# One small SBUF tile made 64 bytes wider, in a channel attention and rational feed-forward kernel

## The chip, the cores and the metric

The kernel runs on one core of a Trainium2 chip. The metric is device time in microseconds (us), from one execution of the program; several runs are compared by their median.

## The reference

There are 4 batches of 6080 tokens with 256 channels. The first part is an attention over channels, the second a feed-forward layer whose activation is a quotient of two polynomials:

```python
qn = q / (norm(q, axis=1) + 1e-06)            # q, k, v: (4, 6080, 256), norms over the tokens
kn = k / (norm(k, axis=1) + 1e-06)
s  = kn.transpose(0, 2, 1) @ qn / tau         # (4, 256, 256)
a  = exp(s - s.max(-1)); a /= a.sum(-1) + 1e-09
x  = (v @ a).reshape(24320, 256)
h  = x @ w_in                                 # w_in: (256, 2048)
P  = a0 + a1*h + a2*h**2 + a3*h**3
Q  = 1 + abs(b0)*abs(h) + abs(b1)*h**2
out = (P / (Q + 1e-06)) @ w_out               # w_out: (2048, 256)
```

All is float32.

## The kernel before

The attention matrix of a batch is multiplied into w_in once per batch (`fuse`), so that each token needs two products only: `mm1`, from the 256 channels of v to the hidden units, and `mm2`, from the hidden units to 256 outputs. To keep float32 accuracy, each operand is split into a high and a low part, and each product is the sum of three: high by high, high by low, low by high.

Tokens are worked on in groups of 512, the last group of a batch has 448. The 2048 hidden units are cut into 8 pairs of 2 x 128. For one group and one pair (`pair`), mm1 is two runs of 6 matmuls: `whi` by `vhi`, `whi` by `vlo`, `wlo` by `vhi` for each half of the 256 channels, into one bank of the PSUM tile `hx`. ACT, DVE and POOL make the rational function of hx out of it with `d`, `uu` and `r`, in two parts `ghi` and `glo` (tiles `gh`, `gl`). mm2 then multiplies these with `w_out_hi` and `w_out_lo` and adds into the PSUM tile `acc`, 12 matmuls per group and pair. In the profile a matmul is written as output, stream and weights: `hx<-vhi,w` streams vhi past the weights in w. The low weights have the tiles `w2`, which the profile's names show as `w` too.

Beside that PE makes the products of k and q of the next batch (`hx<-kq`, `acc<-kq`) and the fused weights (`hx<-w_in_sb,kq`), both in plain float32, where one product is two matmuls in the profile.

Each engine's instructions stand in an order that a planner (`Planner`) works out when the kernel is built, from costs and from the due times in `LAG` and `TIME`. The addresses play no part in it.

Tiles in SBUF are made at the end, once all sizes are known: `buf` notes the greatest size of each tag in `homes`, and the loop over `homes.items()` (L1140 to L1144) makes the tiles in the order in which the tags were first used. In the built program they lie one after the other, each rounded up to 32 bytes per partition. Six of them are very small: n2, e, rn, st and two of sm, 16 bytes each, so 32 with rounding. They lie between orow and w:

| tiles, in this order | bytes of one | start before | residue of 128 |
|---|---|---|---|
| w_in_sb, w_out_hi, w_out_lo | 16384 | 17888 (first) | 96 |
| d, uu, r, kq, sq, orow | 4096 | 67040 (first) | 96 |
| n2, e, rn, st, sm, sm | 16 | 132576 (n2) | 96, 0, 32, 64, 96, 0 |
| w (8), w2 (8) | 2048 | 132768 (first) | 32 |
| vst, vhi, vlo | 4096 | 165536 (vst) | 32 |
| sacc | 2048 | 186016 | 32 |
| ssq, gh, gl | 4096 | 188064 (ssq) | 32 |

So mm1 has its weights and its streams at residue 32, and mm2 has weights at residue 96 and streams at 32. All offsets of the operands inside these tiles are multiples of 512 bytes.

Of the kernel before, what the change touches and what calls it, by code (L numbers as in the profile page):

```python
# [297 lines left out]
def tile_channel_attention_rational_ffn(  # L298
# [841 lines left out]
    for tag, width in homes.items():  # L1140
        if tag in ("hA", "hB"):
            continue
        home, n = (ps, SLOTS["hA" if tag == "hx" else tag]) if tag in ("hx", "acc") else (sb, SLOTS[tag])
        homes[tag] = [home.tile([P, width], F32, name=f"{tag}{i}") for i in range(n)]  # L1144
    for s in plans[0][1]:
        s.fn()
# [39 lines left out]
```

## Time and profile before

| | us |
|---|---|
| median of 3 runs | 2421.33 (2420.75 to 2424.07) |
| profiled execution, its own time | 2420.11 |
| its span, first to last instruction | 2418.2 |
| PE busy | 2370.3 |
| DVE busy | 2156.7 |
| ACT busy | 2067.5 |
| POOL busy | 1839.3 |

All times of instructions below come from the profiled execution. A matmul's length in the profile is longer than the distance to the next one's start, since matmuls overlap; how long PE needs per matmul is read from the distance of starts.

### The profile page before, as it was taken

How to read it: one execution, taken by the hardware profiler on the slowest of the kernel's cores; microseconds unless marked ns; L12 is line 12 of the kernel's file. 1: busy time of each engine (PE TensorE's matmuls, PEld its weight loads, DVE VectorE, ACT ScalarE, POOL GpSimd, SP SyncE). 2: the span in 40 equal slices, each digit the busy share in tenths (PEclk: the TensorE clock that was granted, in tenths of full speed). 3: DMA queues.
4: the chain of work that ended last, by engine and by line, in shares of the span. 5: the costliest groups of instructions: out<-in, count | busy, mean ns of one | idle time of the engine just before them, and what ended most of it. 6: DMA issues, size and time to landing. Idle time of an engine off the chain costs nothing.

```text
span 2418.2 us, 30382 instructions
## 1 busy us (share of the span) xinstructions
PE 2370.3 (98%) x10312; PEld 1938.8 (80%) x10312; DVE 2156.7 (89%) x2627; ACT 2067.5 (85%) x2072; POOL 1839.3 (76%) x1427
## 2 busy tenths in 40 slices
PE   7899999999999999999999999999998999999998
PEld 5677888888888888888888888888887788888887
DVE  5889999997878799999987889999996999999998
ACT  4789999986767799999986689999997999999996
POOL 7797777778779977777768987777774777777775
PEclk9899999999999999999999999999999999999999
DMA  9532121136467511211146731211111121111201
GB/s 299 159 71 36 18 36 18 18 57 150 87 142 152 119 26 22 31 18 28 25 89 140 169 61 23 30 18 28 24 18 18 20 33 18 27 27 18 32 12 19
DMA packets 455862, 141.15 MB, mean 58 GB/s; under 512 B 395888, under 2 KB 445040, under 8 KB 455696
## 3 DMA queue, kind: packets, MB, share of 16 engines
q1 hardware_dynamic: 447152, 108.04, 21.6%
q0 software_dynamic: 8544, 31.07, 7.2%
q8 instruction: 83, 1.36, 0.2%
q14 instruction: 83, 0.68, 0.1%
HBM read 83.10 MB, written 24.90 MB: 45 GB/s over the span
## 4 chain that ended last, share of the span: by engine, by line
PE 89%; ACT 4%; DVE 2%; issue 2%; DMA 2%; POOL 1%; SPq 0%; DVEq 0%; ACTq 0%; POOLq 0%
PE hx L83 47%; PE acc L83 42%; ACT d L83 2%; ACT r L83 1%; DVE hx L83 1%; ACT uu L83 1%; SPq L83 0%; DVE orow L83 0%; DMA vst<-in_v_dram 0%; DMA d<-in_moe_w_in_dram 0%; DVE gl L83 0%; DVE gh L83 0%; DMA d<-in_q_dram 0%; DMA kq<-in_q_dram 0%; DMA kq<-in_k_dram 0%
## 5 line engine op out<-in xcount | busy, mean ns | idle before, releaser
L83 POOL TENSOR_TENSOR d<-d,gh 128x512 f32<-128x512 f32 (+1 forms) x768 | 978.1, 1303 | 418.7 <-DVE gh L83 414.9
L83 PE MATMUL hx<-vhi,w 128*128 128x512 f32 (+1 forms) x3072 | 1052.6, 391 | 3.8 <-DVE gl L83 2.9
L83 PEld LDWEIGHTS hx<-vhi,w 128*128 128x128 f32 x3072 | 577.5, 188 | 131.5 <-DVE gl L83 5.7
L83 DVE SCALAR_TENSOR_TENSOR hx<-hx,fast,d 128x512 f32<-128x512 f32 (+1 forms) x768 | 566.2, 745 | 61.3 <-POOL d L83 60.2
L83 PE MATMUL hx<-vlo,w 128*128 128x512 f32 (+1 forms) x1536 | 600.1, 391 | 0.0
L83 ACT ACTIVATE uu<-hx,fast 128x1024 f32<-128x1024 f32 (+1 forms) x384 | 422.7, 1101 | 155.5 <-PE hx L83 155.3
L83 POOL TENSOR_SCALAR d<-d,ones,fast 128x1024 f32<-128x1024 f32 (+1 forms) x384 | 467.5, 1220 | 109.6 <-ACT r L83 103.1
L83 DVE TENSOR_TENSOR gl<-hx,r 128x512 fp32r<-128x512 f32 (+1 forms) x768 | 518.1, 678 | 32.7 <-PE acc L83 5.3
L83 DVE SCALAR_TENSOR_TENSOR gh<-hx,fast,r 128x1024 fp32r<-128x1024 f32 (+1 forms) x384 | 485.7, 1265 | 58.1 <-ACT r L83 48.9
L83 DVE SCALAR_TENSOR_TENSOR hx<-uu,fast,hx 128x1024 f32<-128x1024 f32 (+1 forms) x384 | 487.6, 1270 | 35.8 <-ACT d L83 19.6
L83 PE MATMUL acc<-gh,w_out_hi 128*128 128x512 f32 (+1 forms) x1536 | 487.6, 399 | 5.9 <-DVE gh L83 3.3
L83 PE MATMUL acc<-gl,w_out_hi 128*128 128x512 f32 (+1 forms) x1536 | 481.5, 395 | 1.8 <-DVE gl L83 1.8
L83 PE MATMUL acc<-gh,w_out_lo 128*128 128x512 f32 (+1 forms) x1536 | 479.4, 393 | 0.0
L83 ACT ACTIVATE d<-hx 128x1024 f32<-128x1024 f32 (+1 forms) x384 | 387.5, 1009 | 78.6 <-PE hx L83 76.3
L83 ACT ACTIVATE r<-d,fast 128x1024 f32<-128x1024 f32 (+1 forms) x384 | 438.9, 1144 | 11.0
L83 ACT ACTIVATE r<-r 128x1024 f32<-128x1024 f32 (+1 forms) x384 | 403.5, 1052 | 8.3
L83 ACT ACTIVATE d<-d 128x1024 f32<-128x1024 f32 (+1 forms) x384 | 403.3, 1051 | 7.1
L83 PEld LDWEIGHTS acc<-gh,w_out_hi 128*128 128x128 f32 x1536 | 285.8, 188 | 79.2 <-DVE orow L83 16.4
L83 PEld LDWEIGHTS acc<-gl,w_out_hi 128*128 128x128 f32 x1536 | 288.6, 188 | 67.4 <-DVE gl L83 3.4
L83 PEld LDWEIGHTS acc<-gh,w_out_lo 128*128 128x128 f32 x1536 | 289.2, 188 | 65.8
L83 PEld LDWEIGHTS hx<-vlo,w 128*128 128x128 f32 x1536 | 288.7, 188 | 63.5
L83 PE MATMUL hx<-kq 128*128 128x256 f32 (+1 forms) x592 | 137.0, 386 | 12.7 <-DVE fast L83 7.4
(118 smaller groups left out, 1120.9 us busy)
## 6 DMA issues: line engine op xcount, KB each, us to landing
ssq<-sq POOLq DMA_DIRECT2D x54, 512.0 KB, 5.2
vst<-in_v_dram SPq DMA_DIRECT2D x176, 128.0 KB, 4.1
out_dram<-orow SPq DMA_DIRECT2D x176, 128.0 KB, 3.4
kq<-in_k_dram SPq DMA_DIRECT2D x75, 256.0 KB, 4.1
kq<-in_q_dram SPq DMA_DIRECT2D x75, 256.0 KB, 4.4
d<-in_moe_w_in_dram SPq DMA_DIRECT2D x8, 512.0 KB, 5.8
ssq<-sq POOLq DMA_DIRECT2D x6, 448.0 KB, 5.3
r<-in_k_dram SPq DMA_DIRECT2D x9, 256.0 KB, 5.6
```

What stands on the lines that cost most here:

```text
L83: ins = op(*args, **kwargs)
```

## The change

The tile n2 gets 16 more float32 elements per partition, 64 bytes. Nothing reads or writes them.

```diff
@@ -1141,6 +1141,8 @@
         if tag in ("hA", "hB"):
             continue
         home, n = (ps, SLOTS["hA" if tag == "hx" else tag]) if tag in ("hx", "acc") else (sb, SLOTS[tag])
+        if tag == "n2":
+            width += 16
         homes[tag] = [home.tile([P, width], F32, name=f"{tag}{i}") for i in range(n)]
     for s in plans[0][1]:
         s.fn()
```

Every tile behind n2 starts 64 bytes later: w at 132832, vst at 165600, ssq at 188128, all at residue 96 of 128, as are the tiles ahead of n2, which stay. Of the small tiles e, rn, st and the two of sm go to 64, 96, 0, 32 and 64. Modulo 64 no tile's start changes. The instructions of every engine and their order are the same as before.

## Rows read from the trace of the kernel before

**Rows 1.** The page: span, busy time, clock, chain that ended last.

```profile
span 2418.2 us, 30382 instructions
PE 2370.3 (98%) x10312; PEld 1938.8 (80%) x10312; DVE 2156.7 (89%) x2627; ACT 2067.5 (85%) x2072; POOL 1839.3 (76%) x1427
...
PEclk9899999999999999999999999999999999999999
...
PE hx L83 47%; PE acc L83 42%; ACT d L83 2%; ACT r L83 1%; DVE hx L83 1%; ACT uu L83 1%; SPq L83 0%; DVE orow L83 0%; DMA vst<-in_v_dram 0%; DMA d<-in_moe_w_in_dram 0%; DVE gl L83 0%; DVE gh L83 0%; DMA d<-in_q_dram 0%; DMA kq<-in_q_dram 0%; DMA kq<-in_k_dram 0%
```

**Rows 2.** That chain in time order: start us, length us, what, instructions.

```profile
1185.09 1.40 PE acc L83 x6
1186.49 1.39 PE hx L83 x6
...
1190.40 2.80 PE acc L83 x12
1193.21 2.75 PE hx L83 x12
```

**Rows 3.** PE groups by shape: what, count | busy us, mean ns | idle.

```profile
L83 PE MATMUL hx<-vhi,w 128*128 128x512 f32 x2816 | 968.2, 393 | 1.6 <-DVE w L83 0.9 <-DVE gl L83 0.7
L83 PE MATMUL hx<-vlo,w 128*128 128x512 f32 x1408 | 553.1, 393 | 0.0
L83 PE MATMUL acc<-gh,w_out_hi 128*128 128x512 f32 x1408 | 449.0, 400 | 0.9 <-DVE orow L83 0.6
L83 PE MATMUL acc<-gl,w_out_hi 128*128 128x512 f32 x1408 | 443.2, 396 | 0.0
L83 PE MATMUL acc<-gh,w_out_lo 128*128 128x512 f32 x1408 | 442.4, 395 | 0.0
```

**Rows 4.** Weight loads by shape, columns as in rows 3.

```profile
L83 PEld LDWEIGHTS hx<-vhi,w 128*128 128x128 f32 x3072 | 577.5, 188 | 131.5 <-DVE gl L83 5.7 <-DVE w L83 1.3
...
L83 PEld LDWEIGHTS acc<-gl,w_out_hi 128*128 128x128 f32 x1536 | 288.6, 188 | 67.4 <-DVE gl L83 3.4
```

**Rows 5.** PE timeline near 1195 us: start us, length us, what, count.

```profile
1195.57 0.39 PE L83 MATMUL hx<-vhi,w 128*128 128x512 f32 x1
1195.79 0.63 PE L83 MATMUL acc<-gl,w_out_hi 128*128 128x512 f32 x2
```

**Rows 6.** The same view near 690 us, short group, then q-k products.

```profile
688.40 0.57 PE L83 MATMUL acc<-gh,w_out_hi 128*128 128x448 f32 x2
...
691.64 3.61 PE L83 MATMUL hx<-kq 128*128 128x256 f32 x16
695.09 1.89 PE L83 MATMUL hx<-w_in_sb,kq 128*128 128x256 f32 x8
```

**Rows 7.** The same view near 1214 us, first matmuls of a short group.

```profile
1214.17 0.36 PE L83 MATMUL hx<-vhi,w 128*128 128x448 f32 x1
...
1215.39 0.62 PE L83 MATMUL acc<-gh,w_out_hi 128*128 128x512 f32 x2
```

**Rows 8.** Groups of ACT, DVE and POOL by shape, columns as in rows 3.

```profile
L83 ACT ACTIVATE sq<-kq 128x1024 f32<-128x1024 f32 x17 | 17.8, 1052 | 5.3 <-DMA kq<-in_q_dram 2.7 <-DVE acc L83 2.6
...
L83 ACT ACTIVATE ssq<-kq 128x1024 f32<-128x1024 f32 x2 | 2.1, 1062 | 0.0
...
L83 DVE TENSOR_TENSOR gl<-hx,r 128x512 fp32r<-128x512 f32 x704 | 479.7, 684 | 31.8 <-PE acc L83 5.3 <-DVE hx L83 0.5
...
L83 DVE TENSOR_TENSOR w_in_sb<-hx,uu 128x512 f32<-128x512 f32 x4 | 2.8, 688 | 0.1
...
L83 POOL TENSOR_TENSOR orow<-sq,orow 128x1024 f32<-128x1024 f32 x13 | 31.0, 2387 | 16.0 <-ACT sq L83 15.8
L83 POOL TENSOR_TENSOR ssq<-sq,ssq 128x1024 f32<-128x1024 f32 x9 | 22.3, 2474 | 1.0 <-ACT sq L83 0.9
```

**Rows 9.** Each engine's busy time in the stretch 200 to 600 us.

```profile
core 0: us, PE busy (x) PEld busy (x) DVE busy (x) ACT busy (x) POOL busy (x), PEclk, DMA share, GB/s
200.00:600.00 400.00, 399.90 (x1727) 323.62 (x1726) 372.48 (x437) 355.28 (x343) 308.46 (x241) 1.00 0.24 45
```

## The prediction

> **What bounds the kernel now.** I read the page first. PE is busy 2370.3 of 2418.2 us, and the chain that ended last lies on PE for hx (47%) and acc (42%); its clock stands at 9 tenths or more in all but the second slice, so at the level of 2.4 GHz [rows 1]. What PE does per matmul is therefore the time of the kernel, and every matmul that gets shorter or longer counts until another engine is late. Between 200 and 600 us PE has 399.90 us of work in 400 and DVE, the next, 372.48 [rows 9], so there is room for about 7% before DVE would be the bound.
>
> Second I read the chain in order of time, where I take the spacing of matmuls from the start of one to the start of the next. A mm2 run (acc) of 12 takes 2.80 us and one of 6 takes 1.40, both 233 ns each. A mm1 run (hx) of 6 takes 1.39, which is 231.7, and one of 12 takes 2.75 [rows 2]: taking the first six at 1.39 leaves 1.36 for the second six, 226.7 each. The reader is to see that mm1 falls into a shorter beat once it follows itself, and that mm2, twelve in a row, doesn't. 512 columns at 2.4 GHz are 213.3 ns, so 13 to 20 ns of every matmul are something else, and that is what this change could touch.
>
> The counts: 2816 + 1408 = 4224 mm1 matmuls of 512 columns and three times 1408, 4224 too, of mm2 [rows 3]. The profile's length of one reaches over the next one's start, so only differences of it are used: rows of mm1 have a mean of 393, those of mm2 without waits 395 and 396 (400 with a few waits in it).
>
> **The change part by part.** It adds and removes no instruction, wait or transfer, and the order on each engine is the same; n2 is used through a slice, so VectorE still works on 4 of its columns. What moves is the start of every tile from e on, by 64 bytes. Before, mm1 loads its weights (w, w2) from residue 32 and streams vhi, vlo from residue 32; mm2 loads w_out from 96 and streams gh, gl from 32. After, all of these are 96. So for mm1 the pair stays equal and both move; for mm2 the pair was 64 apart and becomes equal.
>
> *Weight loads.* At residue 32 (w) a load takes 188 ns and at residue 96 (w_out_hi) 188 ns [rows 4], both under a stream of residue 32. Cost of the move: 0, from two groups of 3072 and 1536.
>
> *The pair 96 under 32.* It exists before at one more place than inside mm2: at the handover, the last matmul of a mm1 run streams from 32 while the weights of mm2 are loaded from 96. There it is 1195.57 to 1195.79, 220 ns by rounded starts, not 233 [rows 5]. The unequal pair by itself doesn't make the spacing of mm2.
>
> *The same pair with other widths.* On the group of 448 tokens mm2 has 16 matmuls, eight rows of two, from 688.40 to 691.64: 202.5 ns [rows 6]; six of mm1 go from 1214.17 to 1215.39: 203.3 [rows 7]. The pairs are 96/32 and 32/32 as above, and the unequal one isn't the slower. And mm1 with one and the same pair has both 231.7 and 226.7 [rows 2]. So the spacing follows what ran before and how wide the matmul is, and I find no row in which the residue of 128 alone goes with it. I take 0 for PE.
>
> *What no row shows* is a stream of 512 columns from residue 96. From below the nearest are the products of q and k, both operands in kq at 96: 16 matmuls from 691.64 to 695.09, 215.6 ns [rows 6]; each takes 256 columns in that time, so half the bytes, and is a far bound. From above it is the spacing of mm2, 233.3, for mm1 as well. Mean spacing now: mm2 233.3 [rows 2]; mm1 lies 2.5 lower, as its mean of 393 does under 395.5 [rows 3], so about 230.8, and both together 232. With the lower bound 8448 x (232 - 215.6) = 139 us would go, with the upper one 4224 x 2.5 = 11 us would come. I take no change, since weight load, handover and the 448 group, three nearer rows, give it.
>
> *The other engines.* They write and read the moved tiles too (gh, gl, vhi, vlo, w, ssq). ACT squares kq into sq (96) in 1052 ns and into ssq (32) in 1062; DVE writes gl (32) in 684 and w_in_sb (96) in 688; POOL adds into orow (96) in 2387 and into ssq (32) in 2474 [rows 8]. The ends are within 4%, on engines that PE almost never waits for, so their cost is put at 0. What hides it is PE's own 399.90 in 400 [rows 9]; without that cover DVE's 0.6% would be 2 us in 400.
>
> The sum is 0 on the profiled 2420.11 us (span 2418.2 and 1.9 around it). The median of the runs is 2421.33, with 3.3 us from the lowest to the highest; I forecast 2421. A difference under 0.2% (4.8 us) can't be told from none here.
>
> **A rule against this.** The products of q and k, the one long run with both operands at 96, have the tightest spacing of all [rows 6]. The Trainium skill, TensorE: Matmul & The Clock Gate, section Back-to-back issue gap, gives 518 cycles for 512 columns by themselves, which at 2.4 GHz is 215.8 ns; the trace has that for kq and not for mm1 and mm2. If equal residues of 96 were what gives it, the sum by the Trainium skill's figure would be near the third rival's.
>
> **The rivals.** *First, mm2 falls into mm1's short beat, and mm1 no longer leaves it.* For it: mm2 is the one kind with unequal residues and the one kind that never gets the beat in a run of 12 [rows 2]. Against it: the handover and the 448 group. Time: 4224 x (233.3 - 226.7) = 28 us for mm2 and 4224 x (230.8 - 226.7) = 17 us for mm1, 45 together, 2376; DVE's 372.48 in then 392 still fits, though some waits would come up, and a part of it alone is as likely, so 2376 to 2412.
>
> *Second, slower: weights at 96 are what keeps mm2 from the beat, and now mm1's are there too.* It decides if a load from 96 matters only once the weights in use came from 96 as well; this is the handover's way out, since there only one of the two did. Place: every mm1 run. Price: mm1 at mm2's spacing, the 11 us from above, 2432; a beat yet longer than mm2's, which no run here shows, would add more. Against it: loads of 188 ns at either residue.
>
> *Third, all 8448 go at 215.6:* 139 us less, 2282, where DVE (2156.7 busy) [rows 1] would begin to be late. Against it: kq's stream needs only half the bytes.
>
> That the tiles would not move at all is no rival, since the addresses of the built program show them moved.
>
> **How the numbers follow.** No change 0.53, first rival 0.26, third 0.01, second 0.20. So faster by over 0.2% is 0.27, the same 0.53, slower 0.20. The likeliest alone is 2416 to 2426. The range takes in most of the first rival's 2376 to 2412 and the second's 2432 with 6 us on top for a longer beat: 2384 to 2438. That leaves out the lowest edge of the first, the third, and a slower beat than any run of before has: about 1 in 10.
>
> **What would show it.** If I am right, the chain has mm2 runs of 12 at 2.80 and mm1 runs of 6 and 12 at 1.39 and 2.75, and the groups have means of 393 and 395 to 396. The first rival shows as 12 of acc in about 2.72 and means of 389 throughout; the second as 12 of hx in 2.80; the third as a mean near 378. The weight loads stay at 188 in each. I am wrong if a run of 12 mm2 at the same granted clock is not within 0.02 us of 2.80.

## The result, and the profile after

The changed kernel takes 2395.58 us (median of 4 runs, 2392.04 to 2396.64) against 2422.04 of before (median of 4 now, one run more than the 2421.33 above), a ratio of 0.9887 (95% interval 0.987 to 0.9905): 26 us faster. I had forecast no change; what came is the first rival, faster, inside the stated range. The profiled execution took 2392.04 us. Its page, with busy times, clock and the shares of the chain that ended last:

```profile
span 2390.1 us, 30382 instructions
PE 2333.6 (98%) x10312; PEld 1936.2 (81%) x10312; DVE 2151.3 (90%) x2627; ACT 2062.4 (86%) x2072; POOL 1836.2 (77%) x1427
...
PEclk8999999999999999999999999999999999999999
...
PE 67%; ACT 15%; DVE 10%; issue 5%; DMA 1%; POOL 1%; SPq 0%; DVEq 0%; POOLq 0%; ACTq 0%
PE hx L83 37%; PE acc L83 30%; ACT d L83 6%; ACT r L83 5%; DVE hx L83 4%; ACT uu L83 3%; DVE gh L83 2%; DVE orow L83 2%; DVE gl L83 1%; POOL d L83 1%; DMA r<-in_q_dram 0%; DMA out_dram<-orow 0%; ACT L83 0%; DMA kq<-in_q_dram 0%; DMA d<-in_moe_w_in_dram 0%
```

Set beside [rows 1], PE has 36.7 us less to do, at the same clock and with the same 10312 matmuls. The chain leaves PE more often: 67% of the span is PE now, where before hx and acc alone made 89%.

The chain in order of time (start, length, what, matmuls), beside [rows 2]:

```profile
1183.18 1.36 PE hx L83 x6
1184.54 2.72 PE acc L83 x12
1187.26 2.72 PE hx L83 x12
...
1196.78 1.36 PE acc L83 x6
```

A run of 12 mm2 (acc) has gone from 2.80 to 2.72 us, 226.7 ns per matmul, and a run of 12 mm1 from 2.75 to 2.72; a run of 6 takes 1.36 whichever it is. So both kinds are in the short beat, and the first six of an mm1 run after an mm2 run are no longer slower than the next six. The groups by shape, beside [rows 3], and the weight loads, beside [rows 4]:

```profile
L83 PE MATMUL hx<-vhi,w 128*128 128x512 f32 x2816 | 961.2, 390 | 2.2 <-DVE gl L83 1.1 <-DVE w L83 0.9
L83 PE MATMUL hx<-vlo,w 128*128 128x512 f32 x1408 | 548.1, 389 | 0.0
L83 PE MATMUL acc<-gh,w_out_hi 128*128 128x512 f32 x1408 | 440.7, 394 | 9.1 <-DVE orow L83 9.0
L83 PE MATMUL acc<-gl,w_out_hi 128*128 128x512 f32 x1408 | 434.5, 390 | 0.0
L83 PE MATMUL acc<-gh,w_out_lo 128*128 128x512 f32 x1408 | 434.2, 389 | 0.0
```

```profile
L83 PEld LDWEIGHTS hx<-vhi,w 128*128 128x128 f32 x3072 | 577.1, 188 | 125.6 <-DVE gl L83 8.7 <-DVE w L83 1.3
...
L83 PEld LDWEIGHTS acc<-gl,w_out_hi 128*128 128x128 f32 x1536 | 287.9, 188 | 60.8 <-DVE gl L83 3.7
```

Means of 389 and 390 everywhere (394 where waits are in it), and weight loads of 188 ns as before. That is what the prediction had listed as the sign of the first rival.

PE's 36.7 us less became 28.1 us less span (2418.2 to 2390.1). The other 8.6 us are nearly all one wait that grew by 8.5, that of PE for DVE's transpose of acc (columns: who for whom, us, times, longest). Before, and after:

```profile
PE acc L83 <- DVE orow L83: 2.3, 4, 0.6
```

```profile
PE acc L83 <- DVE orow L83: 10.8, 33, 0.7
```

acc has one place in PSUM, so the first mm2 of a group can't start before DVE has carried the last group's acc out. At one such edge PE's timeline and DVE's are (start, length, what, count):

```profile
257.90 0.62 PE L83 MATMUL acc<-gl,w_out_hi 128*128 128x512 f32 x2
258.36 0.39 PE L83 MATMUL hx<-vhi,w 128*128 128x512 f32 x1
...
259.49 0.39 PE L83 MATMUL hx<-vhi,w 128*128 128x512 f32 x1
260.47 0.73 PE L83 MATMUL acc<-gh,w_out_hi 128*128 128x512 f32 x2 [0.59 <-DVE orow L83]
```

```profile
258.51 0.76 DVE L83 SCALAR_TENSOR_TENSOR hx<-hx,fast,d 128x512 f32<-128x512 f32 x1
259.18 1.24 DVE L83 STREAM_TRANSPOSE orow<-acc 128x1024 f32<-128x1024 f32 x1
260.34 0.65 DVE L83 TENSOR_TENSOR gl<-hx,r 128x512 fp32r<-128x512 f32 x1
```

PE has one mm1 run to do in between; DVE starts the transpose after it has finished an `hx<-hx,fast,d`, and its 1.24 us end after that run. In the kernel before, at the same edge, the last mm2 ended at 261.26 us and the transpose began at 261.46, 0.20 later; here the two are 258.52 and 259.18, 0.66 apart. With 226.7 ns per matmul PE has come further ahead of DVE's order than it was, and waits.

### The profile page after: what moved, and what is told of

Read it like the earlier page. It is cut to its first block, busy times and chain, and to the rows that moved or that the text cites. A ratio compares the mean times of both kernels' runs of the same rounds, so it can differ in the third digit from the quotient of the medians.

```text
span 2390.1 us, 30382 instructions
## 1 busy us (share of the span) xinstructions
PE 2333.6 (98%) x10312; PEld 1936.2 (81%) x10312; DVE 2151.3 (90%) x2627; ACT 2062.4 (86%) x2072; POOL 1836.2 (77%) x1427
## 3 DMA queue, kind: packets, MB, share of 16 engines
q8 instruction: 83, 1.36, 0.2%
## 4 chain that ended last, share of the span: by engine, by line
PE 67%; ACT 15%; DVE 10%; issue 5%; DMA 1%; POOL 1%; SPq 0%; DVEq 0%; POOLq 0%; ACTq 0%
PE hx L83 37%; PE acc L83 30%; ACT d L83 6%; ACT r L83 5%; DVE hx L83 4%; ACT uu L83 3%; DVE gh L83 2%; DVE orow L83 2%; DVE gl L83 1%; POOL d L83 1%; DMA r<-in_q_dram 0%; DMA out_dram<-orow 0%; ACT L83 0%; DMA kq<-in_q_dram 0%; DMA d<-in_moe_w_in_dram 0%
## 5 line engine op out<-in xcount | busy, mean ns | idle before, releaser
L83 PE MATMUL acc<-gh,w_out_hi 128*128 128x512 f32 (+1 forms) x1536 | 478.7, 393 | 14.2 <-DVE orow L83 10.8
L83 PE MATMUL acc<-gl,w_out_hi 128*128 128x512 f32 (+1 forms) x1536 | 472.6, 389 | 1.8 <-DVE gl L83 1.8
L83 PE MATMUL acc<-gh,w_out_lo 128*128 128x512 f32 (+1 forms) x1536 | 470.7, 388 | 0.0
```

Of the source, the lines that this page charges most:

```text
L83: ins = op(*args, **kwargs)
```

## The experiments

Each edit is given by its changed lines against the kernel before. `{'n2': 16}.get(tag, 0)` makes the tile n2 wider by 16 float32, 64 bytes, and no other; `fast` is a small tile of constants ahead of all wide tiles, which are those of 2048 bytes and more. Nothing else moves but the starts of the tiles behind the widened one. Three theories stood at the start: the residues of a pair (weights and stream of one matmul) must be equal; the stream must start at 96; all weights that follow each other must start at one residue. A later question was whether the period is 128 or 256 bytes. To read the results, these are the starts modulo 256, counted from the built programs, and what came out. The distance is the weights' start less the stream's, modulo 256; each ratio is to runs of the kernel before taken beside that kernel.

| kernel | mm1 weights, stream | mm2 weights, stream | distance mm1, mm2 | us | ratio to before (95%) |
|---|---|---|---|---|---|
| before | 160, 160 | 224, 160 | 0, 64 | 2422.04 | 1 |
| changed | 224, 224 | 224, 224 | 0, 0 | 2395.58 | 0.9887 (0.987 to 0.9905) |
| all at 32 | 32, 32 | 32, 32 | 0, 0 | 2394.87 | 0.9888 (0.9872 to 0.9905) |
| swapped | 224, 224 | 32, 224 | 0, 64 | 2421.78 | 0.9999 (0.9989 to 1.0008) |
| mm2 alone | 160, 160 | 224, 224 | 0, 0 | 2407.84 | 0.9936 (0.9919 to 0.9953) |
| both apart | 224, 32 | 224, 32 | 192, 192 | 2404.94 | 0.993 (0.9913 to 0.9947) |
| 128 apart | 96, 96 | 224, 96 | 0, 128 | 2417.4 | 0.9982 (0.9972 to 0.9991) |
| all at 0 | 0, 0 | 0, 0 | 0, 0 | 2392.55 | 0.9879 (0.9863 to 0.9896) |
| 32 apart | 192, 192 | 224, 192 | 0, 32 | 2417.11 | 0.9985 (0.9976 to 0.9995) |
| 64 apart | 224, 160 | 224, 160 | 64, 64 | 2434.72 | 1.0054 (1.0037 to 1.0071) |

**All at 32.**

```diff
-    fast = const.tile([P, 16], F32, name="fast")
+    fast = const.tile([P, 32], F32, name="fast")
+        width += {'n2': 16}.get(tag, 0)
```

> All wide tiles start at residue 32 of 128 instead of 96. Theory of equal residues (a matmul keeps the short beat of 226.7 ns where its weights and its stream start at the same residue of 128): about 2395 us, runs of 12 mm2 in 2.72 us. Theory of the absolute residue (a stream that starts at 96 is what gives the beat): mm2 stays at 233, runs of 12 in 2.80, about 2422 us or a little more. Theory of uniform weights (the beat is kept while all weights that follow each other start at one residue): 2395 us, as the first.

Runs of 12, from the chain:

```profile
1185.72 2.72 PE acc L83 x12
1188.44 2.72 PE hx L83 x12
```

The whole gain is there with no stream at 96. The absolute residue is out.

**Swapped.**

```diff
-    fast = const.tile([P, 16], F32, name="fast")
+    fast = const.tile([P, 32], F32, name="fast")
```

> The two residues exchanged: mm1 has weights and streams at 96, mm2 has weights at 32 and streams at 96. Equal residues: mm2 stays without the beat, runs of 12 in 2.80 us, mm1 loses it for six matmuls after each mm2 run, about 2422 us. Absolute residue of the stream: all streams are at 96, so all in the beat, about 2395 us. Uniform weights: weights change between 96 and 32, about 2422 us.

```profile
1193.34 2.80 PE acc L83 x12
1196.14 2.75 PE hx L83 x12
1199.36 1.39 PE hx L83 x6
```

All streams are at 96 of 128, yet the times are those of before to 0.1%: 2.80 for mm2, 2.75 and 1.39 for mm1. With "all at 32" beside it, what counts is a relation between starts; these two runs leave open whether it is that of a pair or that of weights to weights.

**mm2 alone.**

```diff
+        width += {'sacc': 16}.get(tag, 0)
```

> Only ssq, gh and gl move to 96: mm1 has weights and streams at 32, mm2 has both at 96. Equal residues: both kinds in the beat, 2395 us if the handovers cost nothing, up to 2405 if they do; mm2 runs of 12 in 2.72 us, mm1 runs of 6 in 1.36. Absolute residue of the stream: mm2 in the beat and mm1 not, about 2405 us. Uniform weights: no gain, about 2422 us.

```profile
1185.76 1.39 PE hx L83 x6
1187.15 2.76 PE acc L83 x12
1189.91 2.73 PE hx L83 x12
```

Both pairs are equal in themselves, but mm1's tiles lie 64 bytes away from mm2's. The result, 2407.84, is half the gain, and above the 2405 that I had given the theory of equal pairs at most: a run of 12 takes 2.76 or 2.73, and 6 mm1 again 1.39. There is a gain though the weights are not uniform. Equal pairs give the beat, and each change of kind loses it for some matmuls: by the starts in the trace the mean spacing is back at 226.7 ns after about ten.

**Both apart.**

```diff
+        width += {'n2': 16, 'vst': 16}.get(tag, 0)
```

> Weights of mm1 and mm2 at 96, streams of both at 32. Equal residues: neither has the beat, mm1 and mm2 runs of 12 in 2.80 us, 4224 x 2.5 ns more than before, about 2432 us. Absolute residue of the stream: streams at 32 as before, about 2422 us. Uniform weights: all weights at 96, so all in the beat, about 2395 us.

```profile
1185.05 2.75 PE acc L83 x12
1187.80 2.75 PE hx L83 x12
```

All three theories miss: 2404.94, not 2432, 2422 or 2395. Both kinds are at 229 ns, one as the other, though each pair is 64 apart modulo 128, with which mm2 took 233 before. Modulo 256 the distance is 192 here and was 64 there, which led to the next runs.

**128 apart.**

```diff
+        width += {'n2': 48}.get(tag, 0)
```

> All wide tiles at residue 96 of 128 as in the changed kernel, but mm1's tiles and mm2's streams at 96 of 256, mm2's weights at 224 of 256, so that mm2's pair is 128 bytes apart. Theory of a period of 128: as the changed kernel, about 2395 us, runs of 12 mm2 in 2.72 us. Theory of a period of 256 (the pair has to agree modulo 256): mm2 leaves the short beat, between 229 and 233 ns per matmul, 2405 to 2422 us.

```profile
1197.78 2.80 PE acc L83 x12
1200.58 2.74 PE hx L83 x12
```

mm2 is back at 2.80 although all wide tiles begin at 96 of 128, as in the changed kernel. The period is not 128; in the changed kernel the tiles agree modulo 256 too, and here they don't.

**All at 0.**

```diff
-    fast = const.tile([P, 16], F32, name="fast")
+    fast = const.tile([P, 24], F32, name="fast")
+        width += {'n2': 16}.get(tag, 0)
```

> All wide tiles at residue 0 of 128. If only the equality of residues counts: about 2395 us, as the changed kernel and as with all at 32. If a start on a full line of 128 or 64 bytes gives something of its own: lower than 2390 us, runs of 12 in less than 2.72 us.

```profile
1185.34 2.72 PE acc L83 x12
1188.06 2.72 PE hx L83 x12
```

The same 2.72. A start at a multiple of 256 bytes gives the runs nothing of its own; the time, 2392.55 (2391.46 to 2393.33), is not under 2390, and the interval of its ratio overlaps that of the changed kernel.

**32 apart.**

```diff
+        width += {'n2': 8}.get(tag, 0)
```

> mm1's weights and streams and mm2's streams at residue 64, mm2's weights at 96: mm2's pair 32 bytes apart. Any unequal pair of mm2 costs the beat: mm2 at 229 to 233 ns, mm1 in transients after it, 2405 to 2422 us. If only bit 6 of the address counts (32 against 96 before): 64 and 96 share that bit, so all in the beat, about 2395 us.

```profile
1196.09 2.80 PE acc L83 x12
1198.89 2.75 PE hx L83 x12
```

mm2 at 2.80 again, so 32 bytes are enough to lose the beat; the theory of bit 6 is out. mm1 is less disturbed than before (2.75 or 2.73), and most of mm2's price is kept. The time, 2417.11, lies inside the 2405 to 2422 expected for any unequal pair.

**64 apart.**

```diff
+        width += {'n2': 16, 'vst': 48}.get(tag, 0)
```

> As with both kinds apart (weights at residue 96, streams at 32), but the weights lie 64 bytes above the streams modulo 256, as mm2's did before, and not 192. Period of 256: both kinds at 233 ns, about 2432 us. Period of 128: no difference to the 192 apart, 229 ns and about 2405 us; then mm2's 233 in the kernel before comes from its alternation with mm1, whose pair was another.

```profile
1204.56 2.80 PE acc L83 x12
1207.36 2.80 PE hx L83 x12
```

This differs from "both apart" by 128 bytes under the streams and nothing else, and takes 30 us more: 2434.72 against the 2432 expected with a period of 256. At 64 apart both kinds stand at 233.3, at 192 apart at 229. So mm2's spacing in the kernel before comes from its own pair, not from alternating with mm1. All weights start at one residue here, and no run is in the beat: uniform weights are out as well.

The same starts counted modulo 512 show that 256 is enough. The distances of mm1 and mm2 are then 0 and 256 in the changed kernel, 448 and 192 in "both apart", 320 and 64 in "64 apart": 256 bytes from each other in all three, and both kinds have the same spacing each time.

**The transpose sooner.** In the planner's finished order, each transpose of acc is exchanged with the DVE step before it, where that is `hx<-hx,fast,d` (in the changed kernel, and the same in the kernel before). `turns` holds the transposes and `rests` those steps; the lines that collect them are left out here:

```diff
-        return plan.order(), first
+        order = plan.order()
+        for turn in turns if quick else ():
+            i = order.index(turn)
+            j = max(x for x in range(i) if order[x].eng == "DVE")
+            rest = order[j]
+            if rest in rests and not any(x in rest.after for x in order[j + 1 : i + 1]):
+                del order[j]
+                order.insert(i, rest)
+        return order, first
```

> The changed kernel, and on DVE the transpose of acc into orow stands one instruction sooner (ahead of hx<-hx,fast,d instead of behind it) wherever the two follow each other. If the new wait of PE for that transpose is what gave back part of the gain: the 10.8 us of PE acc <- DVE orow shrink to 2 us or less, and the time is about 2386 us. If the wait only stands where another would end as late (the delayed hx<-hx,fast,d makes gl late): about 2395 us, with a new wait of PE for gl.

> The same move of the transpose in the kernel before, without the wider tile. There the wait is 2.3 us, so at most 2 us can go: 2420 to 2422 us. If it gains 9 us here too, the wait did not come with the change.

> The changed kernel once more, beside these two on the same chip: 2392 to 2397 us.

It lost: 2408.8 us, ratio 0.9947 (0.9933 to 0.996) to before, where the changed kernel beside it had 2394.62, ratio 0.989 (0.9875 to 0.9905): 14 us dearer, and neither the 2386 nor the 2395 that I had put down. In the kernel before it cost 17 us: 2438.37, 1.0067 (1.0054 to 1.0081), not the 2420 to 2422 expected. PE's waits and those of its weight loads show why, first with the transpose sooner, then the weight loads' in the changed kernel:

```profile
PE hx L83 <- DVE gl L83: 9.9, 37, 3.0
...
PE acc L83 <- DVE orow L83: 2.3, 4, 0.6
```

```profile
PEld hx L83 <- DVE gl L83: 40.8, 96, 3.4
```

```profile
PEld hx L83 <- DVE gl L83: 9.7, 16, 3.4
```

The wait for the transpose did shrink, from 10.8 us to what it was before the change. But `hx<-hx,fast,d` and the `gl` behind it come about 1.2 us later, the length of the transpose, mm1 waits for the hx place that this gl gives free, and the weight loads' wait for gl goes from 9.7 to 40.8 us. Summed over the distances of starts of 512-column matmuls, the changes from mm1 to mm2 take 8.7 us less than in the changed kernel, but mm1 takes 9.7 us more inside its runs and 11.0 more at the changes from mm2 to it. So the 8.5 us given back are a wait for DVE that this exchange only turns into a dearer one. Whether another order wins them was not tried.

## Why the prediction was right and wrong

The range held the result because it had been drawn to take in the first rival; the forecast itself, no change at 0.53, and the steps that led to it were wrong.

- *What bounds the kernel*: right. The time followed PE's spacing, and DVE still fitted.
- *The short beat*: the reading of [rows 2] was right, and the size too: 226.7 ns is what runs of both kinds went to.
- *Weight loads, 188 ns at either residue*: true and beside the point. They are 188 in every row after as well; what changes is not the load's own length.
- *The pair 96 under 32 at the handover*: this step failed. I took one spacing of 220 ns at [rows 5] as a test of the unequal pair. The view rounds starts to 10 ns; by the trace's own starts the spacing is 226 ns, that of the run before it, and the next one, inside mm2, is 236. Over all 503 such handovers without a wait the mean is 228.9. "Mm2 alone" shows that what a matmul's spacing is depends on the ones before it: one matmul right after a run in the beat doesn't show where a run of such pairs settles. "64 apart" shows that: put mm1 on the unequal pair throughout, and it goes to 233.3.
- *The 448 group*: failed as evidence too. The readings were right, but in the changed kernel, where mm2's pair is equal, mm2's matmuls of 448 columns have a mean spacing of 204.2 ns by the trace's starts, against 203.3 before. At 448 columns equal pairs bring nothing, so the group can't speak for 512.
- *"mm1 with one and the same pair has both 231.7 and 226.7"*: true, and read the wrong way round. The 231.7 was mm1 recovering from mm2's unequal pair, so it was part of the price.
- *No change at 0.53*: the sum's term for PE was put at 0 and was 36.7 us of PE time, 28.1 of span. The first rival priced it at 45 us for a full gain, which was too much: it took 233.3 and 230.8 ns for all matmuls, while the spacing at a change of kind, 228.9 and 229.7 by the trace's starts, had been shorter all along. It left 2376 to 2412 for a part of the gain, with waits that would come up; they did, for 8.6 us.
- *The second rival* (weights at 96 keep mm2 from the beat): out by the result itself, since all weights start at 96 now and both kinds are in the beat, and by "swapped", where mm2's weights are at 32 and its runs still take 2.80. *The third* (215.6 as for q and k): no run of equal pairs got under 226.7, at any of the starts 0, 32, 96, 160, 192 and 224 modulo 256. The Trainium skill, TensorE: Matmul & The Clock Gate, section Back-to-back issue gap, gives 518 cycles for 512 columns by themselves, 215.8 ns at 2.4 GHz; no run of 512 columns here, each with a weight load under it, reached that. Why is not shown: the products of q and k have a weight load under each too and stand at 215.6 [rows 6], with 256 columns of plain float32.

## What to carry to other kernels

Where PE is the bound and streams 512 columns of fp32r with a new weight load under each, look at the spacing of starts in long runs by kind, and place weights and streams of all kinds at one residue modulo 256; a pad of 64 bytes was worth 1.1% here. A single spacing at the border between two kinds is no test of a pair, since the spacing carries over; take runs of 12. Then look for the wait that the faster engine runs into.

## What the hardware showed that I had not expected

With 512 columns at the granted clock of 2.4 GHz, the spacing settles by the weights' start less the stream's, modulo 256: 226.7 ns at 0, 233 at 32, 64 and 128, 229 at 192. The 233 at 64 is a mean: in the trace's starts 231 and 236 ns come in turn. At 32 and 128 only mm2's pair was tried, and no other distance at all. Equal pairs at two different starts still lose the beat at each change of kind. The Trainium skill, TensorE: Matmul & The Clock Gate, section Step-by-step: what each phase is for, gives PE two independent read ports, one for the stream and one for the weights; the runs show that the spacing depends on both starts together, and do not show whether the two reads meet at the ports or in the memory behind them. Why the period is 256 bytes stays open.
